# Loading and transposing the next group's rows earlier in a feed-forward loop, and beginning six conversions instead of eight in its first group

## The chip, the cores and the metric

The kernel runs on one core of one Trainium2 chip. The metric is the device time of one execution in microseconds, as a median of several runs. A core has TensorE (matmuls and transposes, results in PSUM), VectorE, ScalarE and GpSimd for the rest, and SyncE, which here issues the DMA transfers. Each engine works through its own queue in order and waits on semaphores of the others.

## The reference

Three stages, one after the other, all in float32. The first is a recurrent attention (four batches, eight heads, 768 positions, head size 40) whose output is 3072 rows of 320. The second sends each row to one of eight experts of size 320 x 1024 x 320 and adds the result to the row. The third, in which the change lies, is a dense feed-forward over all rows:

```
h = x @ w_in                      # 3072 x 320 times 320 x 2048
g = h            where h >= 1
    0            where h <= -1
    (h + 1)^2/4  between
out = g @ w_out                   # 3072 x 2048 times 2048 x 320
```

The two weights come as float64 numbers.

## The kernel before

Products are kept near float32 precision by splitting each operand into a rounded high part and a rest, and adding three products (high x high, high x rest, rest x high).

The feed-forward treats the 3072 rows in six groups of 512 (`TG`, `NGRP`). The hidden size is cut into 16 blocks of 128. It makes two passes (`a`) over the six groups: the first with blocks 0 to 7, the second with 8 to 15. So there are twelve visits (`v`) of eight steps each (`j`). One step does, in the order in which it is written:

* TensorE: eight matmuls of 512 columns (L1309) give the hidden block in a bank of PSUM (three such banks);
* TensorE: `dstage2` for the block of three steps ago, twelve matmuls of 320 columns (L1284 to L1286) into four banks that collect a group's output; after a group's eighth block the four results are copied out and stored to `yhalf` (first pass), or added to it and stored to `out`; since it lags three steps, this falls into step 2 of the next visit;
* VectorE clips the block to [-1, 1] (L1315), ScalarE squares (L1316), VectorE takes the maximum with the block (L1320), ScalarE rounds to the high part `gh` (L1321), GpSimd makes the rest `gl` (L1322).

Besides, two other kinds of work are woven into the first pass.

*The next group's rows.* `load_g` has SyncE load 512 rows (640 KB) of `x2b`, the expert stage's output in device memory, into a buffer of which there is one (`rows4`; the second pass uses it for `load_half`). For the loads it waits until all scattered writes of the expert stage have landed. The rows are then transposed in three sets of four (`turn_tile_g`, L1251, for k = 0, 1, 2) into a PSUM bank of which there is one (`psT`), and each set is split by `part_g`: ScalarE rounds the high part `dxh` (L1257), VectorE subtracts to get the rest `dxl` (L1259; for k = 2 L1261). In a step's matmuls the third set is needed from the seventh on. The first group's rows come about differently, before the loop.

*Conversion of the float64 weights.* A job (`convert`) turns one tile of `w_in` or `w_out` into its two parts. `launch` begins a job by issuing its load (into `cv_st`, three buffers); `advance(stage)` lets all jobs that stand at this stage go one further. Stage 0 is two ScalarE instructions (L957, L958), 1 one of VectorE (L961), 2 another (L963), 3 two of VectorE (L965, L966), 4 one of ScalarE (L968) and one of GpSimd (L969), 5 one of VectorE (L971) and one of GpSimd (L972). By the order of the calls a job begun in step s goes through stage 0 in step s + 1, through 1 to 4 in s + 2 and through 5 in s + 3. There are 40 jobs; 14 are begun in the expert stage (`EARLY`), 26 here. The first pass needs the first 20 of all, in the order of their blocks.

Order: within an engine the instructions stand as the program has them (`manual_schedule`). Issues of DMA on SyncE can move ahead of others that wait.

Of the kernel before, what the change touches and what calls it, by code (L numbers as in the profile page):

```python
# [54 lines left out]
def mlstm_moe_ffn_kernel(  # L55
# [26 lines left out]
    def psS(name):  # L82
        return bank("psS", 3, name)
# [4 lines left out]
    def psT(name):  # L88
        return bank("psT", 1, name)
# [900 lines left out]
    def launch():  # L990
        if conv_jobs:
            g = convert(*conv_jobs.pop(0))
            next(g)
            flying.append([g, 0])

    def advance(stage):

        for c in list(flying):
            if c[1] == stage:
                c[1] += 1  # L1000
                if next(c[0], 1) == 1:
                    flying.remove(c)
# [237 lines left out]
    def load_g(g):  # L1240
        new_g(g)
        x = Xg[g]
        x["b"] = dp.tile([128, 4, DM], F32, name="xg2", tag="rows4", bufs=1)
        after("x2", nc.sync.dma_start(x["b"], x2b[g * TG:(g + 1) * TG, :].rearrange("(t p) c -> p t c", p=128)))

    def turn_tile_g(g, q, k):
        x = Xg[g]
        if q == 0:
            x["t"][k] = psT(f"dx{g}_{k}")
        r = 128 if k < 2 else 64  # L1250
        nc.tensor.transpose(x["t"][k][:r, q * 128:(q + 1) * 128], x["b"][:, q, k * 128:k * 128 + r], ident)  # L1251

    def part_g(g, k):
        x = Xg[g]
        t, xh, xl = x["t"][k], x["h"], x["l"]
        r = 128 if k < 2 else 64
        nc.scalar.activation(xh[:r, k, :], t[:r], AF.Copy)  # L1257
        if k < 2:
            nc.vector.tensor_tensor(xl[:, k, :], t, xh[:, k, :].bitcast(F32), op=ALU.subtract)  # L1259
        else:  # L1260
            nc.vector.tensor_tensor(xh[64:, k, :], t[:64], xh[:64, k, :].bitcast(F32), op=ALU.subtract)  # L1261
# [11 lines left out]
    def load_half(g):  # L1273
        half_y[g] = dp.tile([128, 4, DM], F32, name="yhb", tag="rows4", bufs=1)
        nc.sync.dma_start(half_y[g], rows_of(yhalf, g))

    def dstage2(g, f, gh, gl, tiles=(0, 1, 2, 3)):
        a = f // FH
        if f % FH == 0:
            yst[g] = [psY(f"dy{g}_{a}_{q}") for q in range(4)]  # L1280
        ys = yst[g]
        for q in tiles:
            sl = slice(q * 128, (q + 1) * 128)
            nc.tensor.matmul(ys[q][:, :DM], gh[:, sl], woh[:, f, :], start=(f % FH == 0), stop=False)  # L1284
            nc.tensor.matmul(ys[q][:, :DM], gh[:, sl], wol[:, f, :], start=False, stop=False)  # L1285
            nc.tensor.matmul(ys[q][:, :DM], gl[:, sl], woh[:, f, :], start=False, stop=(f % FH == FH - 1))  # L1286
        if f % FH == FH - 1:
            for q in tiles:
                ot = dp.tile([128, DM], F32, name="ot", bufs=4)
                if a:  # L1290
                    nc.vector.tensor_tensor(ot, ys[q][:, :DM], half_y[g][:, q], op=ALU.add)
                elif q % 2:
                    nc.scalar.activation(ot, ys[q][:, :DM], AF.Copy)
                else:
                    nc.vector.tensor_copy(ot, ys[q][:, :DM])
                nc.sync.dma_start((out if a else yhalf)[g * TG + q * 128:g * TG + (q + 1) * 128, :], ot)

    prev = []
    for v in range(2 * NGRP):
        a, g = divmod(v, NGRP)  # L1300
        xh, xl = Xg[g]["h"], Xg[g]["l"]
        for j in range(FH):
            f = a * FH + j
            fs = slice(f * 128, (f + 1) * 128)
            mm = [(wih[:, 0, fs], xh[:, 0]), (wil[:, 0, fs], xh[:, 0]), (wih[:, 1, fs], xh[:, 1]), (wil[:, 1, fs], xh[:, 1]),
                  (wih[:, 0, fs], xl[:, 0]), (wih[:, 1, fs], xl[:, 1]), (wih[:, 2, fs], xh[:, 2]), (wil[:, 2, fs], xh[:, 2])]
            hp = psS(f"dh{g}_{f}")
            for n, (w, x) in enumerate(mm):
                nc.tensor.matmul(hp, w, x, start=(n == 0), stop=(n == 7))  # L1309
            if len(prev) == 3:  # L1310
                dstage2(*prev.pop(0))
            u = dp.tile([128, TG], F32, name="du", bufs=3)
            gh = dp.tile([128, TG], F32R, name="gh", bufs=5)
            gl = dp.tile([128, TG], F32R, name="gl", bufs=5)
            nc.vector.tensor_scalar(u, hp, -1.0, 1.0, op0=ALU.max, op1=ALU.min)  # L1315
            nc.scalar.activation(u, u, AF.Square, bias=half, scale=0.5)  # L1316
            if a == 0:
                for stage in (1, 5, 2, 0):
                    advance(stage)
            nc.vector.tensor_tensor(u, u, hp, op=ALU.max)  # L1320
            nc.scalar.activation(gh, u, AF.Copy)  # L1321
            (nc.vector if (v, j) == (2 * NGRP - 1, FH - 1) else nc.gpsimd).tensor_tensor(gl, u, gh.bitcast(F32), op=ALU.subtract)  # L1322
            if a == 0:
                for stage in (3, 4):
                    advance(stage)
                if g == 0 or j % 2:
                    launch()
                if g + 1 < NGRP:
                    if j == 2:
                        load_g(g + 1)  # L1330
                    if 5 <= j < 8:
                        for q in range(4):
                            turn_tile_g(g + 1, q, j - 5)
                        part_g(g + 1, j - 5)
            elif j == 4:
                load_half(g)
            prev.append((g, f, gh, gl))
# [86 lines left out]
```

## Time and profile before

| | |
|---|---|
| median of 3 runs | 718.83 us (717.49 to 720.84) |
| the profiled execution | 718.89 us, its span 717.1 us |
| mean granted TensorE clock | 0.967 |
| TensorE busy | 668.6 us (93%), 4743 matmuls |
| VectorE busy | 515.8 us (72%) |
| ScalarE busy | 346.4 us (48%) |
| GpSimd busy | 379.0 us (53%) |

The feed-forward begins at about 348 us and lasts to the end. In the rows below, PE is TensorE, DVE VectorE, ACT ScalarE, POOL GpSimd and SP SyncE; L1309 is line 1309 of the kernel. Names such as `du<-dh` say which tile is written from which. A timeline's row may merge several instructions (x4); brackets at its end give the idle time before it and what ended it. The clock is a share of 2.4 GHz.

### The profile page before, as it was taken

The page shows a single profiled execution, that of the slowest core. Times are in us where ns is not written, and L with a number is a line of the kernel's source. Part 1 is how long each engine was busy: PE and PEld are TensorE (multiplying, and loading weights), DVE is VectorE, ACT ScalarE, POOL GpSimd, SP SyncE. Part 2 cuts the span into 40 slices and gives each one's busy share as a digit, 9 for nine tenths or more (in the row PEclk, how much of TensorE's full clock was granted, in tenths as well). Part 3 has the DMA queues.
Part 4 walks back from the last instruction along what each step waited for, and adds up shares of the span by engine and source line. Part 5 has one row for each costly group of instructions (what it writes and reads, how often), then busy time and mean ns, then how long its engine had stood idle before and what let it go on. Part 6 is the DMA issues. An engine that isn't in the chain of part 4 may idle for free. (4 is left out here: it accounts for less than half of the span.)

```text
span 717.1 us, 13220 instructions
## 1 busy us (share of the span) xinstructions
PE 668.6 (93%) x4743; PEld 590.9 (82%) x4744; DVE 515.8 (72%) x1228; ACT 346.4 (48%) x623; POOL 379.0 (53%) x369
## 2 busy tenths in 40 slices
PE   6779989797899999999979999999999999999997
PEld 3657777686799999999778888989899999999997
DVE  8788998999389999998697766767564344344443
ACT  5344444553356566555465555555544333333432
POOL 7354766666257677776376555546463333333331
PEclk8997989799899999999999999999999999999999
DMA  5988878854456665673122230304102022020121
GB/s 162 240 263 221 238 241 232 232 177 133 125 206 212 208 216 184 207 252 114 44 71 70 99 120 22 122 19 136 38 19 74 0 74 74 1 74 33 41 74 37
DMA packets 44744, 91.54 MB, mean 128 GB/s; under 512 B 5004, under 2 KB 30601, under 8 KB 43790
## 3 DMA queue, kind: packets, MB, share of 16 engines
q1 hardware_dynamic: 42574, 86.67, 39.1%
q0 software_dynamic: 2048, 3.93, 1.6%
q8 instruction: 39, 0.64, 0.4%
q14 instruction: 35, 0.29, 0.1%
q10 hardware_dynamic: 48, 0.02, 0.0%
HBM read 71.60 MB, written 21.94 MB: 130 GB/s over the span
## 5 line engine op out<-in xcount | busy, mean ns | idle before, releaser
L1322 POOL TENSOR_TENSOR gl<-du,gh 128x512 fp32r<-128x512 f32 x95 | 123.1, 1295 | 171.5 <-ACT gh L1321 143.3
L1316 ACT ACTIVATE du<-du,half 128x512 f32<-128x512 f32 x96 | 69.5, 724 | 114.2 <-DVE du L1315 114.2
L1309 PE MATMUL dh<-dxh,wih 128*128 128x512 f32 x288 | 115.2, 400 | 6.2 <-DVE dxh L1261 6.2
L1286 PE MATMUL dy<-woh,gl 128*128 128x320 f32 x384 | 118.7, 309 | 0.0
L1285 PE MATMUL dy<-wol,gh 128*128 128x320 f32 x384 | 118.6, 309 | 0.0
L1284 PE MATMUL dy<-woh,gh 128*128 128x320 f32 x384 | 118.3, 308 | 0.0
L1315 DVE TENSOR_SCALAR du<-dh 128x512 f32<-128x512 f32 x96 | 66.0, 688 | 67.9 <-PE dh L1309 65.6
L1309 PE MATMUL dh<-dxh,wil 128*128 128x512 f32 x288 | 113.8, 395 | 0.0
L1320 DVE TENSOR_TENSOR du<-du,dh 128x512 f32<-128x512 f32 x96 | 65.8, 686 | 48.6 <-ACT du L1316 48.5
L1321 ACT ACTIVATE gh<-du 128x512 fp32r<-128x512 f32 x96 | 60.7, 633 | 66.7 <-DVE du L1320 65.7
L665 POOL TENSOR_TENSOR wl<-wst,wh 128x768 fp32r<-128x768 f32 x29 | 53.9, 1859 | 46.9 <-ACT wh L664 46.7
L1284 PEld LDWEIGHTS dy<-woh,gh 128*128 128x128 f32 x384 | 72.2, 188 | 3.6
L1285 PEld LDWEIGHTS dy<-wol,gh 128*128 128x128 f32 x384 | 72.1, 188 | 3.6
L1286 PEld LDWEIGHTS dy<-woh,gl 128*128 128x128 f32 x384 | 72.1, 188 | 0.0
L1309 PEld LDWEIGHTS dh<-dxh,wih 128*128 128x128 f32 x288 | 54.4, 189 | 17.3 <-DVE dxh L1261 8.7
L363 POOL TENSOR_SCALAR_AFFINE_SELECT W<-W 128x512 f32<-128x512 f32 x48 | 31.8, 685 | 61.8 <-ACT W L357 61.7
L1309 PEld LDWEIGHTS dh<-dxh,wil 128*128 128x128 f32 x288 | 54.5, 189 | 8.2
L1309 PE MATMUL dh<-dxl,wih 128*128 128x512 f32 x192 | 59.8, 392 | 0.0
L1022 PE MATMUL hp<-xh,wh 128*128 128x272 f32 x192 | 56.4, 306 | 3.5 <-ACTq L866 3.2
L1022 PE MATMUL hp<-xh,wl 128*128 128x272 f32 x192 | 53.8, 292 | 0.0
L357 ACT ACTIVATE W<-bp 128x512 f32<-128x512 f32 x48 | 25.9, 594 | 37.8 <-PE bp L354 23.3
L1309 PEld LDWEIGHTS dh<-dxl,wih 128*128 128x128 f32 x192 | 36.4, 190 | 8.4 <-DVE dxl L1259 0.2
(233 smaller groups left out, 1544.9 us busy)
## 6 DMA issues: line engine op xcount, KB each, us to landing
wst<-in_wm SPq DMA_DIRECT2D x32, 704.0 KB
kvt<-in_kv SPq DMA_DIRECT2D x12, 648.0 KB
qk<-in_qk SPq DMA_DIRECT2D x22, 320.0 KB
cv_st<-in_win SPq DMA_DIRECT2D x24, 256.0 KB
cv_st<-in_wout SPq DMA_DIRECT2D x16, 320.0 KB
sig<-in_og SPq DMA_DIRECT2D x12, 420.0 KB
x2b<-xr SPq DMA_DIRECT2D x24, 160.0 KB
yhalf<-ot SPq DMA_DIRECT2D x24, 160.0 KB
```

Of the source, the lines that this page charges most:

```text
L363: nc.gpsimd.affine_select(out=Wj, in_=Wj, pattern=[[0, 4], [1, CH]], compare_op=ALU.is_ge, fill=0.0, base=0, channel_multiplier=-1)
L665: (eng or nc.gpsimd).tensor_tensor(wl[:, :768], s[:, :768], wh[:, :768].bitcast(F32), op=ALU.subtract)
L1022: nc.tensor.matmul(hp, w, x, start=(n == 0), stop=(n == 7))
L1284: nc.tensor.matmul(ys[q][:, :DM], gh[:, sl], woh[:, f, :], start=(f % FH == 0), stop=False)
L1285: nc.tensor.matmul(ys[q][:, :DM], gh[:, sl], wol[:, f, :], start=False, stop=False)
L1286: nc.tensor.matmul(ys[q][:, :DM], gl[:, sl], woh[:, f, :], start=False, stop=(f % FH == FH - 1))
L1309: nc.tensor.matmul(hp, w, x, start=(n == 0), stop=(n == 7))
L1315: nc.vector.tensor_scalar(u, hp, -1.0, 1.0, op0=ALU.max, op1=ALU.min)
L1316: nc.scalar.activation(u, u, AF.Square, bias=half, scale=0.5)
L1320: nc.vector.tensor_tensor(u, u, hp, op=ALU.max)
L1321: nc.scalar.activation(gh, u, AF.Copy)
L1322: (nc.vector if (v, j) == (2 * NGRP - 1, FH - 1) else nc.gpsimd).tensor_tensor(gl, u, gh.bitcast(F32), op=ALU.subtract)
```

## The change

In the first pass, `load_g` of the next group goes from step 2 to step 0, and the three sets of transposes with their `part_g` from steps 5, 6 and 7 to steps 2, 4 and 6. In the first group, jobs are begun in steps 0 to 5 instead of 0 to 7; the later groups still begin theirs in steps 1, 3, 5 and 7. So the 26 jobs are begun up to step 7 of group 5 instead of step 3, and to let the last ones finish, `advance` is now called in the second pass too.

```
--- before.py
+++ after.py
@@ -1314,24 +1314,23 @@
             gl = dp.tile([128, TG], F32R, name="gl", bufs=5)
             nc.vector.tensor_scalar(u, hp, -1.0, 1.0, op0=ALU.max, op1=ALU.min)
             nc.scalar.activation(u, u, AF.Square, bias=half, scale=0.5)
-            if a == 0:
-                for stage in (1, 5, 2, 0):
-                    advance(stage)
+            for stage in (1, 5, 2, 0):
+                advance(stage)
             nc.vector.tensor_tensor(u, u, hp, op=ALU.max)
             nc.scalar.activation(gh, u, AF.Copy)
             (nc.vector if (v, j) == (2 * NGRP - 1, FH - 1) else nc.gpsimd).tensor_tensor(gl, u, gh.bitcast(F32), op=ALU.subtract)
+            for stage in (3, 4):
+                advance(stage)
             if a == 0:
-                for stage in (3, 4):
-                    advance(stage)
-                if g == 0 or j % 2:
+                if j % 2 if g else j < 6:
                     launch()
                 if g + 1 < NGRP:
-                    if j == 2:
+                    if j == 0:
                         load_g(g + 1)
-                    if 5 <= j < 8:
+                    if j in (2, 4, 6):
                         for q in range(4):
-                            turn_tile_g(g + 1, q, j - 5)
-                        part_g(g + 1, j - 5)
+                            turn_tile_g(g + 1, q, j // 2 - 1)
+                        part_g(g + 1, j // 2 - 1)
             elif j == 4:
                 load_half(g)
             prev.append((g, f, gh, gl))
```

## Rows read from the trace of the kernel before

**Rows 1.** The page, part 2: VectorE's busy tenths in 40 slices of the span

```profile
DVE  8788998999389999998697766767564344344443
```

**Rows 2.** TensorE's waits from 340 us on: us in total, times, longest

```profile
PE dh L1309 <- DVE dxh L1261: 6.2, 6, 1.3
PE dx L1251 <- DVE dxl L1259: 3.6, 1, 3.6
```

**Rows 3.** The chain of waits, 370 to 560: start us, us, what

```profile
381.94 0.73 PE dh L1309 x2
...
508.08 0.73 PE dh L1309 x2
...
510.56 1.84 PE dh L1309 x8
...
514.16 1.84 PE dh L1309 x8
```

**Rows 4.** TensorE's timeline, 354 and 402 to 407: start us, us, then the instruction

```profile
354.65 0.39 PE L1309 MATMUL dh<-dxh,wih 128*128 128x512 f32 x1
...
402.58 0.48 PE L1309 MATMUL dh<-dxh,wih 128*128 128x512 f32 x1
...
406.62 0.48 PE L1309 MATMUL dh<-dxh,wih 128*128 128x512 f32 x1
```

**Rows 5.** Windows: busy us (instructions) by engine, granted clock, DMA share, GB/s

```profile
375.00:376.00 1.00, 1.00 (x4) 0.81 (x3) 0.97 (x3) 1.00 (x3) 0.41 (x1) 0.50 0.00 0
...
381.00:384.00 3.00, 2.06 (x13) 1.98 (x14) 1.98 (x5) 0.68 (x2) 1.49 (x2) 1.00 0.26 87
```

**Rows 6.** VectorE's timeline, first group: start us, us, then the instruction

```profile
357.72 0.67 DVE L1320 TENSOR_TENSOR du<-du,dh 128x512 f32<-128x512 f32 x1
...
366.02 0.68 DVE L1320 TENSOR_TENSOR du<-du,dh 128x512 f32<-128x512 f32 x1
...
367.52 0.69 DVE L1315 TENSOR_SCALAR du<-dh 128x512 f32<-128x512 f32 x1
...
368.87 1.17 DVE L971 TENSOR_TENSOR cv_b<-cv_b,woh 128x320 f32<-128x320 f32 x1
...
370.19 0.68 DVE L1320 TENSOR_TENSOR du<-du,dh 128x512 f32<-128x512 f32 x1
...
372.47 0.69 DVE L1259 TENSOR_TENSOR dxl<-dx,dxh 128x512 fp32r<-128x512 f32 x1 [0.71 <-ACT dxh L1257]
...
373.07 0.68 DVE L1315 TENSOR_SCALAR du<-dh 128x512 f32<-128x512 f32 x1
...
373.90 0.48 DVE L971 TENSOR_TENSOR cv_b<-cv_b,woh 128x320 f32<-128x320 f32 x1
...
374.60 0.69 DVE L1320 TENSOR_TENSOR du<-du,dh 128x512 f32<-128x512 f32 x1
```

**Rows 7.** GpSimd's timeline, first group, beside L971 at 368.87

```profile
368.72 0.96 POOL L969 TENSOR_TENSOR cv_l<-cv_l,cv_a 128x320 f32<-128x320 f32 x1
```

**Rows 8.** SyncE: waits from 330 to 374, and the loads' issues

```profile
SPq L1244 <- DMA x2b<-x2r,xid: 13.8, 1, 13.8
...
350.40 0.36 SPq L1244 DMA_DIRECT2D xg<-x2b  x1
...
392.68 0.46 SPq L1244 DMA_DIRECT2D xg<-x2b  x1
```

**Rows 9.** DMA from 349 to 357: GB/s in 40 slices of 0.2 us

```profile
GB/s 0 0 0 1 0 0 0 0 0 0 0 0 115 32 19 102 83 243 358 390 390 384 390 410 320 39 0 0 0 0 0 0 0 0 0 0 0 0 0 0
```

**Rows 10.** VectorE's timeline in group 1

```profile
391.61 0.68 DVE L1315 TENSOR_SCALAR du<-dh 128x512 f32<-128x512 f32 x1
...
406.59 0.69 DVE L1320 TENSOR_TENSOR du<-du,dh 128x512 f32<-128x512 f32 x1 [0.39 <-ACT du L1316]
...
408.46 0.69 DVE L1259 TENSOR_TENSOR dxl<-dx,dxh 128x512 fp32r<-128x512 f32 x1 [1.18 <-ACT dxh L1257]
...
409.07 0.68 DVE L1315 TENSOR_SCALAR du<-dh 128x512 f32<-128x512 f32 x1
```

## The prediction

> **What bounds the kernel now.** I read in this order: the page, TensorE's waits, the chain of waits, the timelines of TensorE and VectorE around the longest wait, the granted clock there, then SyncE's queue. From 340 us on, TensorE is idle for ten microseconds in all, and nearly all of it has two causes. Line 1309 waits six times for VectorE's L1261 (0.2 us at the first group's start, the rest at the starts of the five others), and line 1251 waits once, 3.6 us, for L1259 [rows 2]. Both releasers belong to the same work, the splitting of the next group's transposed rows (`part_g`). Elsewhere in the feed-forward TensorE runs step after step without a gap, so a time there is a sum of steps.
>
> A step without transposes takes 514.16 - 510.56 = 3.60 us; a step with four transposes takes 406.62 - 402.58 = 4.04, so 0.44 more [rows 3, 4]. A group of eight steps with its three sets of transposes would take 8 x 3.60 + 3 x 0.44 = 30.1 us. The four groups between 381.94 and 508.08 take 31.53 each [rows 3]. The 1.4 us over is the wait at a group's start: the seventh matmul of its first step needs the third part, which was begun one step before.
>
> The first group is a case of its own. From its fourth step's start (354.65), five steps, three sets of transposes and the 1.39 us to the seventh matmul (six at 0.23) would bring TensorE to the next group's mark at 354.65 + 18.0 + 1.3 + 1.4 = 375.3. It gets there at 381.94 [rows 3, 4]: 6.6 us late. Of that 3.6 and 1.3 are the two waits [rows 2]; the other 1.7 comes with the clock, which was granted at 0.50 (1.2 GHz) after the 3.6 us idle, while the 1.3 us idle left it at 1.00 [rows 5].
>
> Behind these two waits stands VectorE. A step in which each engine converts goes, on VectorE: clip (L1315), conversions, maximum (L1320), conversions, then `part_g` if there is one. Clip to maximum is 370.19 - 367.52 = 2.67 us in a slow step and 374.60 - 373.07 = 1.53 in a quick one; maximum to the next clip is 367.52 - 366.02 = 1.50 without a part and 373.07 - 370.19 = 2.88 with one; maximum to the part's subtraction is 372.47 - 370.19 = 2.28, and that takes 0.69 [rows 6]. A slow step is thus 2.67 + 1.50 = 4.17 us against TensorE's 3.60, and VectorE falls behind through steps 3 to 5, until the second set of transposes finds its only PSUM bank still held.
>
> What makes a step slow is visible: L971 takes 1.17 us at 368.87, when GpSimd's L969 is running (368.72 for 0.96), and 0.48 at 373.90 [rows 6, 7]. After a part the gap of 1.38 us (2.88 - 1.50) lets GpSimd finish first, and the next step is quick.
>
> **The change, part by part.** *Parts in steps 2, 4, 6 (groups 1 to 4 as current group).* The third part now ends more than a step before the next group needs it. The question is whether VectorE gets there. In group 1, clip of step 2 stands at 391.61, behind two copies of finished rows. Without L968 in the even steps, maximum to part is 408.46 - 406.59 = 1.87 and to the next clip 409.07 - 406.59 = 2.48 [rows 10]. Step 2: 391.61 + 1.53 + 2.48 = 395.6. Step 3: + 3.03 = 398.7. Step 4, taken slow: + 2.67 + 2.48 = 403.8. Step 5: + 3.03 = 406.8. Step 6: + 1.53 + 1.87 + 0.69 = 410.9, or 412.1 if it is slow too. TensorE gets to it at 381.94 + 31.53 = 413.5, less the wait of 1.4: 412.1 [rows 3]. So the wait goes, with 0 to 1.2 us over. These start four waits: 4 x 1.44 = 5.8 us gained. Next late would be nothing on that path: the transposes themselves cost what they cost now.
>
> *The same in the first group.* Six jobs are begun in steps 0 to 5 instead of eight in 0 to 7. A job's VectorE work falls in its second and third step after, so steps 3 to 7 carry the same conversions as now; the two jobs left out relieve only the next group's first two steps. What changes is where the parts fall. Maximum of step 2 at 357.72 [rows 6], then by the durations above: clip of step 3 at 357.72 + 2.88 = 360.6; a quick step after a part, maximum 362.1, clip of step 4 at 363.6; slow, maximum 366.3, part, clip of step 5 at 369.2; quick, maximum 370.7, clip of step 6 at 372.2; slow, maximum 374.9, third part 374.9 + 2.28 + 0.69 = 377.9. TensorE, with no wait before (first part done by 360.6, second by 369.2, its sets of transposes due at 362.5 and 370.0), stands at the mark at 375.3 and goes on at 377.9: a new wait of 2.6 us in place of 3.6, 1.3 and the clock. Gain: 381.94 - 377.9 = 4.0 us. Bounds: all steps quick, TensorE's own 375.3, gain 6.6; all steps slow, 360.6 + 4.17 + 5.55 + 4.17 + 2.67 + 2.28 + 0.69 = 380.1, gain 1.8.
>
> The 2.6 us idle lies between 1.3, which kept the clock, and 3.6, which lost it [rows 2, 5]. The price is 0 or 1.7 us; I take 0, because 3.6 is the only idle here that lost it and this one ends a microsecond sooner, and keep 1.7 in the range.
>
> *The load in step 0.* For the first group it is not earlier: SyncE holds it 13.8 us for the last scattered rows and issues it at 350.40 [rows 8]; its bytes have moved by 354.2 (slice 25 of 0.2 us from 349) [rows 9]. The transposes that need it are now due at 354.65 [rows 4]: half a microsecond of cover. If it lands up to 2.6 us later nothing is lost, since TensorE has that much before VectorE's 377.9. On SyncE the loads of the next two jobs may come behind it; the first use of them is a step or more later. In later groups the load's buffer is free once the previous group's step 6 is transposed, and the stores of finished rows that now stand ahead of it (it is issued at 392.68, after them [rows 8]) come two steps after it in the new order. From the issue to landing is 354.2 - 350.4 = 3.8 us, and three steps of 3.6 lie before the transposes.
>
> *Two jobs later, and stepping the conversions in the second pass.* They begin in steps 5 and 7 of the last group, which has no transposes, and end in the second pass's first three steps. There VectorE is busy 3 to 4 tenths [rows 1] and nothing waits for it. Cost 0; without that cover, at most a slow step's excess, 0.6 us each. The weights in question are used first in steps 6 and 7 of that pass. The waits this adds (conversions queued ahead of the maximum in those steps) hold only work that has three steps to finish.
>
> Sum: 718.89 (the profiled execution; its span is 717.1) - 5.8 - 4.0 = 709.1. That execution is 0.06 above the median, so the sum stands for the median too.
>
> **Rivals.** (1) *The first group clears wholly.* If the parts, spread out, keep GpSimd and VectorE from meeting, every step is quick and the gain is 6.6: 718.9 - 12.4 = 706.5. For it: each part is followed by a quick step. Against: the row of slow steps begins before any part.
>
> (2) *VectorE stays slow in the first group.* 1.8 us gained there, and TensorE idle 4.8, so the clock goes as after 3.6: 1.7 back. 718.9 - 5.8 - 0.1 = 713.0. For it: the slow steps in a row [rows 6]. Against: the quick one after a part. The Trainium skill (GPSIMD Engine Reference, section 8, Key points) says that GpSimd shares its SBUF interfaces with VectorE and contends with VectorE's instructions in a two-port mode or with two SBUF inputs. L971 has two SBUF inputs and its two durations agree. By that rule alone, with a GpSimd instruction in every step, no step would be quick and the time would be this rival's; the quick step in the trace is why I give it the smaller chance.
>
> (3) *The wait at the group's start moves into the next part.* Step 2 has the copies as well, VectorE never catches up, and what the starts gain is lost at the second or third set: only the first group's 4.0 stays, less up to 1.7 for the clock: 714.9 to 716.6. For it: the slack of 0 to 1.2 us above. Against: for two steps with one set of transposes TensorE takes 7.6 us, VectorE 3.03 + 1.53 + 2.48 = 7.0 when both are quick and 8.2 when one is slow, so it must be slow nearly every time to fall behind, and not all of a start's 1.44 would come back then.
>
> (4) *Slower: the rows come too late for step 2.* TensorE takes its instructions in order, so transposes without rows stop it. If SyncE still issues the load only behind the stores, at 392.68, they land 3.8 later, at 396.5; the transposes are due at 412.1 - 1.4 - 5 x 3.6 - 1.3 = 391.4. Four waits of 5.1 and the clock's 1.7 each are 27 us: 718.9 - 9.8 + 27 = 736. It decides from 9.8 / 4 = 2.5 us per group. For it: SyncE's queue is in order and the stores wait for their rows. Against: the load stands before these stores in the program. That the change doesn't do what it says is the same case with the wait hidden: the load no earlier and nothing gained.
>
> **How the numbers follow.** Forecast 0.46, rival 1 0.20, rival 2 0.16, rival 3 0.12, rival 4 0.06. A change of 0.5% (3.6 us, so 715.2) is about what a measurement of this kernel can tell from none. Faster: 0.46 + 0.20 + 0.16 and 0.05 of rival 3 = 0.87; same: 0.07; slower: 0.06. The range from 706 to 713.3 holds the first three, with their mixes; the likeliest case alone has 707.9 (one of its two slow steps quick: 2.67 - 1.53 less) to 710.8 (the clock's 1.7 more).
>
> **What would show it.** Right: TensorE's waits list no wait at the starts of groups 2 to 5, and group periods are 30.1; one wait of 2 to 3 us for L1261 at the first group's end, near 375 to 378; no wait of L1251 for L1259; L1244's five loads ahead of each group's stores; TensorE's matmuls in number and duration as before. Wrong: waits of L1251 for a transfer (rival 4) or for L1259 (rival 3), a granted clock of 0.50 after 375 (rival 2), or no wait at all there (rival 1).

## The result, and the profile after

The changed kernel takes 710.72 us (median of 4 runs, 706.55 to 713.05) against 719.84 for the kernel before (4 runs); the ratio is 0.9861, interval 0.9827 to 0.9895. The forecast was 709.1. The profiled execution took 709.59 us, its span 707.7 against 717.1.

TensorE's waits from 330 us on: us in total, times, longest.

```profile
PE dh L1309 <- DVE dxh L1261: 1.5, 2, 1.2
PE dx L1251 <- POOL gl L1321: 0.7, 1, 0.7
```

The five waits at group starts [rows 2] are one, of 1.2 us, and the 3.6 us for L1259 are gone; a new wait of 0.7 stands before the first transposes. (The profile puts it to GpSimd's `gl`, which they do not read; in another run below it names the load.) The chain of waits (start us, us, what), the mark of the first group and then one step of each later group:

```profile
378.35 0.73 PE dh L1309 x2
...
380.83 1.84 PE dh L1309 x8
...
410.92 1.84 PE dh L1309 x8
...
441.00 1.84 PE dh L1309 x8
...
471.08 1.84 PE dh L1309 x8
...
501.16 1.84 PE dh L1309 x8
```

The periods are 30.09, 30.08, 30.08 and 30.08, against 31.53 [rows 3]. The granted clock stays at 1.00 from the first of these rows to the last. VectorE's timeline in the first group; the maximum is L1319 here:

```profile
358.38 0.68 DVE L1319 TENSOR_TENSOR du<-du,dh 128x512 f32<-128x512 f32 x1
...
361.20 0.68 DVE L1315 TENSOR_SCALAR du<-dh 128x512 f32<-128x512 f32 x1
...
362.68 0.69 DVE L1319 TENSOR_TENSOR du<-du,dh 128x512 f32<-128x512 f32 x1
...
364.17 0.69 DVE L1315 TENSOR_SCALAR du<-dh 128x512 f32<-128x512 f32 x1
...
365.52 1.17 DVE L971 TENSOR_TENSOR cv_b<-cv_b,woh 128x320 f32<-128x320 f32 x1
...
366.85 0.67 DVE L1319 TENSOR_TENSOR du<-du,dh 128x512 f32<-128x512 f32 x1
...
369.69 0.68 DVE L1315 TENSOR_SCALAR du<-dh 128x512 f32<-128x512 f32 x1
...
370.52 0.48 DVE L971 TENSOR_TENSOR cv_b<-cv_b,woh 128x320 f32<-128x320 f32 x1
...
371.23 0.69 DVE L1319 TENSOR_TENSOR du<-du,dh 128x512 f32<-128x512 f32 x1
...
372.67 0.68 DVE L1315 TENSOR_SCALAR du<-dh 128x512 f32<-128x512 f32 x1
...
375.38 0.67 DVE L1319 TENSOR_TENSOR du<-du,dh 128x512 f32<-128x512 f32 x1
...
377.61 0.68 DVE L1261 TENSOR_TENSOR dxh<-dx,dxh 64x512 fp32r<-64x512 f32 x1 [0.66 <-ACT dxh L1257]
```

Read it as a beat. With a part, maximum to clip is 361.20 - 358.38 = 2.82. After a part, clip to maximum is 362.68 - 361.20 = 1.48 and 371.23 - 369.69 = 1.54; without a part before it, 366.85 - 364.17 = 2.68 and 375.38 - 372.67 = 2.71, and there L971 takes 1.17 instead of 0.48. That is the sequence of [rows 6], with parts between.

Where the 9.4 us of the span come from, each counted from the feed-forward's first matmul (348.56 before, 349.23 after): the mark of group 1 comes at 33.38 before and 29.12 after, 4.26 gained; four groups gain 31.53 - 30.08 = 1.45 each, 5.8; what follows takes the same in both; and 0.67 is lost ahead of the feed-forward, whose start moves by far more than that between the executions in the table below. 4.26 + 5.8 - 0.67 = 9.4.

This way of counting serves the experiments too. Times of whole runs spread by 1%. In the profiles below, one execution of each kernel, nearly all of that lies ahead of the feed-forward: its first matmul stands anywhere from 345.0 to 356.9 us. The stretch from this matmul to the last instruction repeats within 0.2 us where the waits in the feed-forward are the same:

| kernel | first matmul | span | stretch | first nine steps | next four groups |
|---|---|---|---|---|---|
| before | 348.56 | 717.1 | 368.58 | 35.70 | 31.58, 31.53, 31.47, 31.57 |
| changed | 349.23 | 707.7 | 358.51 | 31.44 | 30.08 each |
| parts_only | 356.86 | 715.4 | 358.51 | 31.44 | 30.08 each |
| launch_only | 349.94 | 718.7 | 368.72 | 35.69 | 31.46, 31.57, 31.69, 31.57 |
| load_only | 345.02 | 713.6 | 368.56 | 35.70 | 31.59, 31.52, 31.45, 31.57 |
| sets_357 | 346.99 | 717.4 | 370.42 | 36.81 | 31.59, 31.66, 31.79, 31.84 |
| sets_456 | 349.35 | 708.9 | 359.53 | 32.47 | 30.08 each |
| no_L969 | 350.87 | 718.8 | 367.98 | 34.50 | 32.24, 31.54, 31.48, 31.49 |
| load_step2 | 350.07 | 739.5 | 389.44 | 31.47 | 38.14, 37.65, 37.62, 37.82 |
| first_235 | 350.57 | 708.7 | 358.09 | 31.04 | 30.08 each |
| after_no_L969 | 345.50 | 702.6 | 357.14 | 30.08 | 30.08 each |

Columns two to six are in us, taken from each trace (starts of the first of a step's eight L1309; the nine steps end where the tenth begins).

### The profile page after: what moved, and what is told of

It reads as the page before. It is cut to its first block, busy times and chain, and to the rows that moved or that the text cites. A ratio compares the mean times of both kernels' runs of the same rounds, so it can differ in the third digit from the quotient of the medians.

```text
span 707.7 us, 13223 instructions
## 1 busy us (share of the span) xinstructions
PE 663.8 (94%) x4744; PEld 588.3 (83%) x4744; DVE 513.4 (73%) x1228; ACT 346.7 (49%) x623; POOL 381.0 (54%) x369
## 5 line engine op out<-in xcount | busy, mean ns | idle before, releaser
L1309 PE MATMUL dh<-dxh,wih 128*128 128x512 f32 x288 | 114.1, 396 | 1.5 <-DVE dxh L1261 1.5
L1309 PE MATMUL dh<-dxh,wil 128*128 128x512 f32 x288 | 113.3, 393 | 0.0
L1319 DVE TENSOR_TENSOR du<-du,dh 128x512 f32<-128x512 f32 x96 | 65.9, 686 | 47.8 <-ACT du L1316 47.8
L1309 PEld LDWEIGHTS dh<-dxh,wih 128*128 128x128 f32 x288 | 54.1, 188 | 10.9 <-DVE dxh L1261 2.2
L1309 PEld LDWEIGHTS dh<-dxh,wil 128*128 128x128 f32 x288 | 54.1, 188 | 8.3
L1309 PE MATMUL dh<-dxl,wih 128*128 128x512 f32 x192 | 59.6, 391 | 0.0
L445 PE MATMUL fin<-wrt,yT 105*128 105x123 f32 x192 | 30.6, 310 | 13.6 <-DVE xr L471 13.6
```

## The experiments

**One part of the change alone.**

```
parts_only:    (changed kernel)
               - if j % 2 if g else j < 6:     + if g == 0 or j % 2:
launch_only:   (changed kernel)
               - if j == 0: load_g(g + 1)      + if j == 2: load_g(g + 1)
               - if j in (2, 4, 6): ...        + if 5 <= j < 8: ...
load_only:     (kernel before)
               - if j == 2: load_g(g + 1)      + if j == 0: load_g(g + 1)
```

> The changed kernel, but with jobs begun in all eight steps of the first group, as before. I compare the feed-forward's own stretch, from its first matmul to the end of the profile: 368.5 us before, 358.5 changed. Theory A (the gain is where the three parts stand: a start's wait of 1.44 us at groups 2 to 5, and VectorE's lag in the first group): steps 3 to 7 carry the same conversions, so the stretch is 358.5, at most 1.5 more because steps 8 and 9 now convert as well while VectorE still lags; time 711 to 712. Rival B (the gain in the first group comes from the two jobs fewer): the waits of the first group come back, stretch 362.5 to 363, time 715.

> The kernel before, with only the beginnings of the conversions changed (steps 0 to 5 of the first group, stepping in the second pass too); load in step 2, sets in steps 5, 6, 7. Theory A: steps 3 to 7 carry the same work, so the wait of 3.6 us for L1259 and the five at the starts stay; stretch 368 to 368.5, time 719. Rival B: the first group's 4 us are gained here, stretch 364.5, time 715.

> The kernel before with only the load moved from step 2 to step 0. Theory A: the load only makes room for the earlier sets and gives nothing by itself: the rows are long there in step 5, stretch 368.5, time 719. Rival C (the queue of SyncE is part of the gain: loads of later jobs no longer stand behind the stores): stretch shorter by 1 us or more.

Ratios to the kernel before: parts_only 0.9845 (0.9781 to 0.9909), launch_only 0.9997 (0.9967 to 1.0027), load_only 1.0007 (0.9974 to 1.0040). TensorE's waits from 340 us on, in this order:

```profile
PE dh L1309 <- DVE dxh L1261: 1.8, 2, 1.6
PE dx L1251 <- DMA xg<-x2b: 0.4, 1, 0.4
```

```profile
PE dh L1309 <- DVE dxh L1261: 6.1, 6, 1.3
PE dx L1251 <- DVE dxl L1259: 3.6, 1, 3.6
```

```profile
PE dh L1309 <- DVE dxh L1261: 6.0, 6, 1.2
PE dx L1251 <- DVE dxl L1259: 3.6, 1, 3.6
```

The stretch of parts_only is the changed kernel's to the hundredth, with all eight beginnings back; its waits are the changed kernel's in kind. The two others keep the kernel before's waits and its stretch within 0.15 us. So rivals B and C fall: where the sets stand carries the whole gain, the load only makes room, and the beginnings of the conversions bring nothing that can be measured.

**How early, and how far apart.**

```
sets_357:  (changed kernel)  sets in j = 3, 5, 7
sets_456:  (changed kernel)  sets in j = 4, 5, 6
```

> The changed kernel with the sets in steps 3, 5, 7: spaced as in the change, but the third begun in the last step, as before. Theory A (what counts for groups 2 to 5 is that the third set is begun a step before its use): the starts' waits of 1.4 us stay, four times; in the first group by the quick and slow steps (clip of step 3 at 359.2 + 0.7, then 2.67 + 2.88, 1.53 + 1.50, 2.67 + 2.88, 1.53 + 1.50, 2.67 + 2.28 + 0.69) the third part ends at 382.7, no bank is waited for, and the mark is where it was before: stretch 367 to 368.5, time 718 to 719. Rival D (the spacing alone does it, since VectorE catches up between sets): stretch 359 to 361, time 711 to 713.

> The changed kernel with the sets in steps 4, 5, 6: the third begun as early as in the change, but no step between the sets. Theory A (what counts is that the third set is a step earlier; the spacing counts only in the first group): groups 2 to 5 start without a wait, periods 30.1; in the first group the second set waits about 3 us for the single bank, as before, and the mark comes 0.5 to 2.2 us later than in the changed kernel (2.2 if the clock falls after that idle): stretch from the first feed-forward matmul to the end 359 to 360.7 (changed 358.5), time 712. Rival D (spacing is what makes it): the first group keeps the whole loss of before, 4.3 us, and later sets wait too: stretch 363 or more.

sets_357 is no faster than the kernel before: ratio 1.0036 (1.0001 to 1.0071). sets_456 is as fast as the change: 0.9840 (0.9780 to 0.9901). TensorE's waits of the first, and the window after its longest (busy us and instructions by engine, granted clock, DMA share, GB/s):

```profile
PE dh L1309 <- DVE dxh L1261: 12.0, 6, 6.3
```

```profile
380.00:382.00 2.00, 1.79 (x5) 1.59 (x6) 0.69 (x2) 0.00 (x0) 0.76 (x1) 0.50 0.00 0
```

All starts wait, as expected, and that of group 1 for 6.3 us: with the sets spaced no bank holds TensorE up, so it meets VectorE's whole lag at once. Its mark comes at 33.22 us from the first matmul, where it was before (33.38), as expected. But the clock falls in this wait, and from the mark to the tenth step it then takes 1.3 us longer, so the first nine steps are 1.1 us longer than the kernel before's; the four groups lose another 0.7. The expectation had no price for either, and the stretch is 1.9 us above its upper bound. The waits of sets_456, and two windows around its longest:

```profile
PE dx L1251 <- DVE dxl L1259: 3.0, 1, 3.0
PE dh L1309 <- DVE dxh L1261: 0.2, 1, 0.2
```

```profile
366.00:369.00 3.00, 0.81 (x6) 0.54 (x4) 2.34 (x5) 1.83 (x4) 1.94 (x3) 1.00 0.05 17
369.00:372.00 3.00, 2.22 (x12) 1.92 (x13) 2.97 (x7) 1.58 (x4) 2.20 (x3) 1.00 0.37 109
```

No start waits, and the periods are 30.08: for groups 2 to 5 it is enough that the third set is a step earlier. The spacing is worth 32.47 - 31.44 = 1.03 us, in the first group alone, where the second set waits 3.0 us for the bank. Rival D falls.

**What makes VectorE slow in the first group.**

```
no_L969:        (kernel before)    - nc.gpsimd.tensor_tensor(l, l, a.bitcast(F32), op=ALU.mult)
after_no_L969:  (changed kernel)   the same
```

> The kernel before without L969, GpSimd's multiplication in each conversion: the rests of the second matrices stay unscaled, so the output is not the reference's. Theory E (a slow step is VectorE's L961 and L971 held off while GpSimd works): L971 in the first group falls from 1.17 to 0.7 or less, VectorE's step from 4.17 to about 3.5, so it no longer falls behind; the wait for L1259 shrinks from 3.6 to about 1.6, the mark comes 2 us earlier, stretch 366.5 (before 368.6); the starts of groups 2 to 5 keep their waits. Rival F (VectorE is slow in these steps for a reason of its own: its queue, ScalarE's square): L971 stays at 1.17 in every second record, stretch 368.6.

VectorE's timeline of no_L969 in the first group, one step without a part:

```profile
364.92 0.68 DVE L1315 TENSOR_SCALAR du<-dh 128x512 f32<-128x512 f32 x1
365.52 0.84 DVE L961 TENSOR_SCALAR cv_a<-cv_a 128x320 f32<-128x320 f32 x1
366.29 0.48 DVE L971 TENSOR_TENSOR cv_b<-cv_b,woh 128x320 f32<-128x320 f32 x1
...
366.92 0.68 DVE L1320 TENSOR_TENSOR du<-du,dh 128x512 f32<-128x512 f32 x1
...
368.37 0.69 DVE L1315 TENSOR_SCALAR du<-dh 128x512 f32<-128x512 f32 x1
```

L971 takes 0.48, and the step 368.37 - 364.92 = 3.45 us instead of 4.17. L961 still takes 0.84, as `gl` remains. That is theory E's reading. The Trainium skill (GPSIMD Engine Reference, section 8, Key points) names instructions with two SBUF inputs among those that contend with GpSimd; L971 has two, and its 0.48 against 1.17 agrees. Nor is it L969 alone that can hold L971 off. In a later step of the same run it is slow again, beside `gl` (399.23 to 400.53), on a tile that took it 0.41 without:

```profile
399.61 1.20 DVE L971 TENSOR_TENSOR cv_b<-cv_b,wih 128x256 f32<-128x256 f32 x1
```

The wait for the bank is 1.5 where 1.6 was expected. TensorE's waits, and a window behind the first start:

```profile
PE dh L1309 <- DVE dxh L1261: 7.2, 6, 2.3
PE dx L1251 <- DVE dxl L1259: 1.5, 1, 1.5
```

```profile
384.00:386.00 2.00, 2.00 (x8) 1.90 (x8) 1.72 (x5) 1.91 (x5) 0.94 (x2) 0.50 0.01 4
```

The mark came 2.1 us earlier (at 31.27), as expected, but the stretch is only 0.6 shorter, where 2 was expected: the first start waits 2.3 us, and the clock falls to 0.50 behind it; 0.9 of the 2.1 us is lost again before the tenth step begins and 0.7 in the next group. The time cannot tell this from nothing (ratio 1.0024, 0.9962 to 1.0087). Left out of the changed kernel, L969 brings no such loss:

> The changed kernel without L969 (the rests of the second matrices stay unscaled, so the output is not the reference's). Theory E (what is left of the first group's loss is VectorE held off by GpSimd in steps 4 and 6): L971 at 0.48 throughout, each of the two slow steps 0.6 to 0.7 shorter, third part done 27.8 us after the first feed-forward matmul instead of 29.1, just when TensorE arrives (27.9): the wait of 1.2 us for it falls to 0.2 or nothing, stretch 357.3 to 357.5 (changed 358.5). Rival H (the rest is the late first set, which keeps TensorE 0.7 us): wait for the third part stays at 1, stretch 358.3 or more.

```profile
PE dh L1309 <- DVE dxh L1261: 0.8, 2, 0.6
```

The mark comes 27.8 us after the first matmul, as expected. Of the 0.8 us listed, 0.6 is at the first group's end, between theory E's 0.2 and rival H's 1: the first set of transposes waited for nothing here, so TensorE reached the mark sooner than expected and still had to wait for VectorE. The stretch is 357.14, 0.2 below what was expected, and the ratio 0.9866 (0.9771 to 0.9962). The first nine steps take 30.08, so 1.36 us of the changed kernel's 31.44 come with L969. The late first set has no part in them: it waits 0.7 us in the changed kernel, 0.4 in parts_only and 0.3 in load_step2 (below), and the nine steps take 31.44, 31.44 and 31.47, since the wait for the third part is shorter by as much (1.2, 1.6 and 1.8). So rival H falls.

**The load's place.**

```
load_step2:  (changed kernel)  - if j == 0: load_g(g + 1)   + if j == 2: load_g(g + 1)
```

> The changed kernel with the load back in step 2, the sets staying in 2, 4, 6: in groups 1 to 4 the load then stands behind the four stores on SyncE. Theory A: transposes of step 2 wait for the rows, four times 5.1 us, and the clock falls after each, 1.7 more: stretch 358.5 + 27 = 385.5, time 738; the first group is not worse (its load waits for the scattered rows in any case). Rival G (DMA issues can move ahead of waiting ones, so the place in the program does not matter): stretch 358.5, time 711.

The ratio is 1.0294 (1.0203 to 1.0384). TensorE's waits, and SyncE's issues around one of the four longest:

```profile
PE dx L1251 <- DMA xg<-x2b: 23.1, 4, 6.0
PE dh L1309 <- DVE dxh L1261: 2.0, 2, 1.8
PE dx L1251 <- PE dh L1309: 0.3, 1, 0.3
```

```profile
388.13 1.79 SPq L1296 DMA_DIRECT2D yhalf<-ot  x4
389.97 0.45 SPq L1244 DMA_DIRECT2D xg<-x2b  x1
```

The load goes out behind the stores, as rival 4 of the prediction has it, though its buffer had been free since the last transposes of the group before, near 372. So rival G falls. The transposes wait 5.8 us each time. With the clock, which falls to 0.50 in each of these waits, a group takes 37.8 instead of 30.08: 7.7, where 6.8 was expected.

**A version.**

```
first_235:  (changed kernel)  in group 0: sets in j = 2, 3, 5, load in j = 2
```

> A version: the changed kernel, but in the first group the sets in steps 2, 3, 5 and its load in step 2, behind the two job loads it need not wait for; later groups as changed. Theory A, by quick and slow steps from the changed kernel's own maximum of step 2 (358.38): third part done at 374.2 instead of 378.3, so the wait of 1.2 us for it goes; but the second set waits 1.1 us for the bank (first part done at 361.3, TensorE there by 359.6 to 360.2): stretch 357.9 to 358.0 against 358.5, time 0.5 us lower at most, not to be told from the changed kernel by times. Rival D (close sets cost more than they give): stretch 359 or more.

```profile
PE dx L1251 <- DVE dxl L1259: 1.4, 1, 1.4
PE dh L1309 <- DVE dxh L1261: 0.2, 1, 0.2
```

The stretch is 358.09: 0.42 us below the change, with the wait for the third part gone and 1.4 us before the second set instead. It beats both kernels in the feed-forward; in the times (ratio 0.9847, 0.9784 to 0.9910) it cannot be told from the change.

## Why the prediction was right, point by point

*Starts of groups 2 to 5.* 5.8 us forecast, 4 x 1.45 measured. VectorE had its third part ready in time in each. The first of them:

```profile
405.11 0.68 DVE L1261 TENSOR_TENSOR dxh<-dx,dxh 64x512 fp32r<-64x512 f32 x1 [1.18 <-ACT dxh L1257]
```

It ends at 405.8 and is needed at 408.55: 2.8 us over, where the forecast had 0 to 1.2. The price of a start was right, but VectorE's time in these groups was forecast too long.

*The first group's recurrence.* Clips of steps 3 to 6 were forecast at 360.6, 363.6, 369.2 and 372.2; measured, less the 0.67 by which this execution's feed-forward began later, 360.5, 363.5, 369.0 and 372.0. The third part was to end at 377.9; it ended at 377.61 + 0.69 - 0.67 = 377.6. The gain was to be 4.0 and was 4.26. Which steps are slow came out right in each case, and the two runs without L969 show why.

*TensorE's wait there.* Forecast 2.6, measured 1.2. The third part was 0.3 earlier, and TensorE reached the mark 1.1 later than the forecast's 375.3: 0.4 because its steps take longer than the sum had them (in parts_only 29.12 less two waits of 1.6 and 0.4 is 27.1 us after the first matmul; the sum had 375.3 - 348.56 = 26.7), and 0.7 in a wait that the sum had put at nothing. I gave the first set half a microsecond of cover, and it started at 356.24, after a wait:

```profile
356.24 0.63 PE L1251 MATMUL dx<-ident,xg 128*128 128x128 f32 x4 [0.73 <-POOL gl L1321]
```

SyncE's issues, and the GB/s from 350 to 358 in slices of 0.2 us:

```profile
351.10 0.36 SPq L1244 DMA_DIRECT2D xg<-x2b  x1
351.51 16.94 SPq L951 DMA_DIRECT2D cv_st<-in_wout  x5
372.17 0.38 SPq L1244 DMA_DIRECT2D xg<-x2b  x1
...
387.26 1.79 SPq L1296 DMA_DIRECT2D yhalf<-ot  x4
```

```profile
GB/s 0 1 0 0 0 0 0 0 0 0 38 70 13 26 83 96 186 173 243 346 397 403 384 403 403 416 422 416 397 422 410 384 243 102 64 13 0 0 0 0
```

The load was issued at 351.10, not earlier, as forecast, but two job loads that had gone out long before (at 318.85 and 330.83 in the kernel before) now stand behind it, and the transfers still run at 400 GB/s five microseconds after its issue. What moves last is theirs: the load's own 512 packets, told by their 1280 bytes, end 4.4 us after its issue, where they had ended after 3.8. That the job loads delay it is argued, and not always so: in after_no_L969, with the same order, they end after 3.8. The cover was misread in any case. The transposes start 0.7 to 0.9 us after the last of these packets, and I had counted nothing for that; with the job loads ahead again, they still wait 0.3 us in load_step2 and 0.2 in first_235. As forecast, such a wait costs nothing while it is shorter than the one that it eats into.

*The clock's 1.7.* I took 0 for the new wait, because it was shorter than the 3.6 that lost the clock. A wait of 2.6 did not occur, so this was not tested as such, and the reason was weak: 2.97 us of idle left the clock at 1.00 in sets_456, while in no_L969 an idle of 1.5 and another of 2.3 lost it. That the 0 came out was partly luck: behind a wait at the mark a fall does count, as sets_357 and no_L969 show. Nor was the 1.7 a term of the old loss on the path: TensorE still waited 1.3 us for VectorE at the mark [rows 2], and without the clock's loss it would have come sooner and waited longer. The windows agree. In the kernel before the clock fell while TensorE still stood idle, in load_only only after it had gone on, and the nine steps took the same 35.70. The first row is the kernel before's, the second load_only's:

```profile
372.00:373.00 1.00, 0.00 (x0) 0.00 (x0) 0.53 (x1) 0.43 (x1) 1.00 (x2) 0.87 0.54 139
370.00:371.00 1.00, 1.00 (x7) 0.82 (x6) 1.00 (x4) 0.70 (x2) 0.22 (x2) 0.84 0.01 2
```

VectorE set the mark in both. This part of my split was a wrong reading that did not enter the sum.

*Edits costed at nothing.* The beginnings in the first group and the stepping in the second pass: shown to be nothing by parts_only and launch_only.

*The rivals.* The first (all steps quick) and the second (all slow) are both refuted by the beat. The third, VectorE not catching up in later groups, did not happen. The fourth's sign, a wait of L1251 for a transfer, showed once, in the first group, where it cost nothing. Its mechanism is real, and its price was a little too low; it did not apply to the later groups because SyncE issues the loads ahead of the stores (372.17 against 387.26 above).

The forecast of 709.1 stands 0.5 below the profiled execution; 0.67 of slower stages ahead and 0.26 of a better first group account for 0.4 of it. That the time came so near is partly luck, as what lies ahead of the feed-forward moves by up to 12 us between the profiles above. The stretch is the fairer test: 368.58 - 9.8 = 358.8 forecast, 358.51 measured.

## What to carry to other kernels

Begin the last piece of prepared work one full step before its first use: a step's distance was worth all of four groups' gain here, the spacing of the pieces only one microsecond in one group. When one queue takes turns with two others, write down its beat from two or three rows (with and without the extra work) and step it forward; it gave the new wait's place and the third part's end within 0.3 us. And move the load with the work: two steps later it would have made the kernel 3% slower.

## What the runs showed of the hardware that was not expected

An idle's length alone does not tell whether TensorE's granted clock falls: 2.97 us kept 1.00 (sets_456), 2.3 us some 6 us after another 1.5 did not (no_L969), and 3.6 us lost it before the idle ended in the kernel before and a microsecond after it in load_only. VectorE's instructions that read one operand from PSUM (clip and maximum, 0.67 to 0.69 in every record of the feed-forward, before and after) keep their duration beside GpSimd, while some with operands only in SBUF stretch: L971 from 0.48 to 1.17, L961 from 0.32 to as much as 0.94.
